# Attention feeding two mixture layers on one core: probabilities turned on VectorE and stored in runs of 32 words, a longer landing time in the written-out order, and the small block's last second products untied

## The chip, the cores and the metric

The kernel runs on one core of one Trainium2 chip. A core has five engines that matter here, each with its own in-order instruction stream: TensorE (PE, with its weight loads PEld), VectorE (DVE), ScalarE (ACT), GpSimd (POOL) and SyncE (SP), which issues nearly all DMAs. The metric is the device time of one execution in microseconds (us); lower is better.

## The reference

```python
q_s = softmax(q, axis=-1); k_s = softmax(k, axis=2)       # 1e-9 added to each sum; q, k, v: [4, 8, 576, 64] float32
attn = einsum('bhsd,bhde->bhse', q_s, einsum('bhsd,bhse->bhde', k_s, v))
x = attn.transpose(0, 2, 1, 3).reshape(2304, 512)
h = x @ w_in                                              # w_in: 512 x 2048, 64-bit floats
g = where(h >= 1, h, where(h <= -1, 0, (h + 1)**2 / 4))
x = g @ w_out                                             # w_out: 2048 x 512, 64-bit floats
p = probs / (probs.sum(-1) + 1e-9)                        # probs: [2304, 4]
out = sum over e of p[:, e] * (relu(x @ w1[e]) @ w2[e])   # w1: [4, 512, 1024], w2: [4, 1024, 512]
```

## The kernel before

**Arithmetic.** Every float32 operand of a large product is split into a high half (a rounded copy, made by `split`, line 479 on ACT or 481 on DVE) and a low half (the rest, line 484 on POOL or DVE). A product of 128 x 512 outputs is three matmuls (`products`, lines 1114 to 1116): low x high, high x low, high x high. I call these three "one product".

**Blocks and passes.** The 2304 tokens are five blocks of 512, 512, 512, 256 and 512. Pass 0 works on blocks 1 and 0, pass 1 on blocks 2 and 4 and on the small block 3. Each pass runs the first layer (kind "a": w_in, w_out) and then the four experts (kind "b": w1, w2), in weight chunks of 128 columns. `ups` emits the first products of a chunk (into `ups_banks`), `gated` or `opened` turns them into the gate (in pass 0, kind "a": lines 1539, 1543 and 1545, on DVE, ACT and DVE), and `downs` emits the second products (into `out_banks`). For pairs of full blocks the products follow Strassen's scheme, with sums of operands in place of the eighth product. In pass 1 the pairs' second products are `second_pairs`; their results are added in `add_pair` (line 1666), combined by `finish_pairs` (`total`), turned by TensorE (line 1718), copied and stored by `turned` (line 1704). The small block's second products are plain ones; `finish_expert` (line 1749) weights them with the probabilities and adds them.

**Probabilities.** `norm_probs` loads the 2304 x 4 probabilities with 36 small DMAs (line 512), normalizes them on DVE (lines 517 to 520), and writes those of blocks 2 and 4 to a DRAM tile `rows_of_p` of 4 rows x 1024, one row for each expert, in 8 DMAs that transpose on the way (line 530). `load_p` (line 469) reads a row of it back, broadcast over 128 partitions, for each expert of pass 1.

**What sets the order.** Each piece of work is a Python generator; `Order.run` simulates the engines with a table of costs and due times and emits the instructions in the order in which that simulation starts them. On the chip each engine then keeps that order, whatever the real times are. `arrival` is the simulation's estimate of when a DMA has landed: a start, the bytes at 360 GB/s, and 0.9 us. DMAs use eight completion counters in turn, and SP issues a DMA only when the last one on the same counter has landed.

Of the kernel before, what the change touches and what calls it, by code (L numbers as in the profile page):

```python
# [8 lines left out]
F32 = mybir.dt.float32  # L9
# [8 lines left out]
P = 128  # L18
# [46 lines left out]
class Order:  # L65
# [6 lines left out]
    HOP = 0.2  # L72
    SPAN = 40.0
# [79 lines left out]
    def arrival(self, issued, size):  # L153

        self.dma_free = max(issued + 0.45, self.dma_free) + size * P / 360e3
        return self.dma_free + 0.9
# [42 lines left out]
def attention_moe_kernel(  # L199
# [48 lines left out]
    CARE = 0.1  # L248
    GATE_DUE = 1
# [14 lines left out]
    def used(g, j):  # L264

        bi, ws = groups[g]
        return (*ws[j], PASS_OF[bi])
# [31 lines left out]
    pn = const.tile([P, NT // P, NE], F32, name="pn")  # L299
    psum_p = const.tile([P, NT // P], F32, name="psum_p")  # L300
# [204 lines left out]
    def norm_probs():  # L505
        start = Event()
        start.set(150.0)
        yield start
        for i in range(NT // P):
            for o, n, rows in token_rows(probs, i * P, P):  # L510
                t = yield SP, 0.65
                nc.sync.dma_start(out=pn[o:o + n, i, :], in_=rows)
        late = Event()
        late.set(t + 3)
        yield late
        t = yield dve(300)
        nc.vector.tensor_reduce(out=psum_p, in_=pn, axis=AX.X, op=ALU.add)
        nc.vector.tensor_scalar(out=psum_p, in0=psum_p, scalar1=EPS, scalar2=None, op0=ALU.add)
        nc.vector.reciprocal(out=psum_p, in_=psum_p)
        nc.vector.tensor_tensor(  # L520
            out=pn, in0=pn, in1=psum_p.unsqueeze(2).to_broadcast([P, NT // P, NE]), op=ALU.mult
        )
        probs_in.set(t)
        i0 = blocks[PASSES[1][0][0]][0] // P
        at = 0
        for bi in PASSES[1][0]:
            b0, n = blocks[bi]
            for i in range(n // P):
                t = yield SP, 0.65
                nc.sync.dma_start(  # L530
                    out=rows_of_p[:, at:at + P].rearrange("e p -> p e"), in_=pn[:, b0 // P + i, :]
                )
                at += P
        rows_in.set(t + 5)
# [135 lines left out]
    def second_of(w):  # L670
        return [u[:, 512:] for u in slot_of[w]] if w[0] == "a" and not is_kept(w) else [
            slot_of[w][:, z * 512:(z + 1) * 512] for z in range(2)]
# [564 lines left out]
    def ups():  # L1237
        for s, (g, j) in enumerate(steps):
# [3 lines left out]
            if w[0] == "b" or is_kept(w):  # L1242
                i, kind = w[3], w[0]
                pair, rest = PASSES[i]
                if bi == pair[0] and j % 2 == 0:
# [8 lines left out]
                    if kind == "b" and i:  # L1254
                        order.care = CARE
# [302 lines left out]

    def downs():
        s0 = 0  # L1560
        for g, (bi, ws) in enumerate(groups):
            n, kind, nj = blocks[bi][1], ws[0][0], len(ws)
# [7 lines left out]
            m = KC if kind == "a" else n // P  # L1570
            place = order_of[bi, kind]
            each = [(j, c) for j in range(nj) for c in range(m)]
            if kind == "a" and bi == PASSES[0][0][1] and g == place[-1]:

                each = [x for x in each if x[0] < 2] + [(j, c) for c in CORDER for j in range(2, nj)]
            ps, left, begun = {}, [m] * nj, [0] * m
            for j, c in each:
                w = used(g, j)
                if left[j] == m:
                    yield s0 + j  # L1580
                    yield ready[w, 1]
                    yield hidden[g, j]
                _, gh, gl = gate_of[g, j]
                bh, bl = second_of(w)
                first, last = begun[c] == 0, begun[c] == nj - 1
                begun[c] += 1
                if first:
                    ps[c] = yield out_banks[c]
                cs = slice(c * P, (c + 1) * P)
                t = yield pe(n if kind == "a" else DM, 3)  # L1590
                if kind == "a":
                    products(ps[c][:, :n], bh[:, cs], bl[:, cs], gh, gl, first, last)
                else:
                    products(ps[c], gh[:, cs], gl[:, cs], bh, bl, first, last)
                if last:
                    order.add((finish_first if kind == "a" else finish_expert)(
                        bi, w, c, ps[c], g == place[0], g == place[-1]), "ffn")
                left[j] -= 1
                if not left[j]:
                    for x in gate_of.pop((g, j))[0]:  # L1600
                        give_gate(x, t)
                    if step_of[w][1] == s0 + j:
                        x = slot_of.pop(w)
                        for x in x if isinstance(x, tuple) else (x,):
                            units.put(x, t)
# [67 lines left out]
    def finish_pairs():  # L1673
# [33 lines left out]
        for c in range(2):  # L1707
            order.add(total(c), "ffn", len(steps))
        for bi, which in ((b2, (1, 3)), (b1, (0, 2))):
            for k in range(blocks[bi][1] // P):  # L1710
# [10 lines left out]
                order.add(turned(bi, k, bank), "ffn", len(steps))  # L1721

    def finish_first(bi, w, c, p, first, last):
# [10 lines left out]
        out_banks[c].put(p, t)  # L1734
# [3 lines left out]
    def finish_expert(bi, w, c, p, first, last):  # L1738
# [13 lines left out]
        out_banks[c].put(p, t)  # L1752
# [11 lines left out]
    with tc.manual_schedule():  # L1764
# [18 lines left out]
        order.add(finish_pairs(), "ffn", len(steps))  # L1783
# [36 lines left out]
```

## Time and profile before

| what | value |
|---|---|
| time, median of 3 runs | 1262.95 us (1262.72 to 1267.39) |
| the profiled execution: its own time | 1272.47 us |
| its span, first to last instruction | 1270.7 us |
| mean granted TensorE clock | 0.984 |
| PE busy | 1219.2 us, 96% of the span |
| DVE, POOL, ACT busy | 820.0, 730.2, 519.8 us |
| chain that ended last | PE 82%, DVE 6%, DMA 5% |

The profiled execution is 9.5 us longer than the median of the runs. Its views are read with its own time in mind. A busy PE counts a matmul that is issued at the lower clock as busy too, so what PE loses is its idle time and what a low granted clock costs.

### The profile page before, as it was taken

The numbers are of one execution on the slowest core, as the hardware profiler recorded it, in microseconds if no ns is written. First come the engines' busy times: TensorE is split into PE (matmuls) and PEld (weight loads), VectorE is DVE, ScalarE is ACT, GpSimd is POOL, SyncE is SP. The second block draws the span as 40 slices with busy tenths as digits, with TensorE's granted clock in tenths as the row PEclk, the third lists the DMA queues.
The fourth block names the chain that finished last, engine by engine and source line by source line (L and its number), as shares of the span: only waits on it lengthen the run. The fifth ranks groups of instructions, "written<-read, shape, count | busy, mean of one in ns | idle before, by whom it ended". The sixth has DMA issues, their size and how long they took to land.

```text
span 1270.7 us, 16472 instructions
## 1 busy us (share of the span) xinstructions
PE 1219.2 (96%) x5802; PEld 1006.3 (79%) x5802; DVE 820.0 (65%) x1246; ACT 519.8 (41%) x957; POOL 730.2 (57%) x680
## 2 busy tenths in 40 slices
PE   9989999599999999999999999999999999999996
PEld 6868888467878778888788888887888888888885
DVE  5977783366655665444651735658777787787786
ACT  4667654343544434332454433625232232233221
POOL 2413231648788878776666737423675576566652
PEclk9989999799999999999999999999999999999999
DMA  8656659316556543534283221513234433443312
GB/s 230 197 176 241 200 200 50 127 41 199 170 191 198 169 157 127 179 126 144 70 258 102 68 86 48 166 51 130 103 133 145 137 133 116 148 135 110 115 42 83
DMA packets 109458, 174.67 MB, mean 137 GB/s; under 512 B 34880, under 2 KB 67648, under 8 KB 109376
## 3 DMA queue, kind: packets, MB, share of 16 engines
q1 hardware_dynamic: 108576, 172.31, 44.6%
q10 hardware_dynamic: 800, 1.31, 0.3%
q8 instruction: 46, 0.75, 0.3%
q14 instruction: 36, 0.29, 0.1%
HBM read 118.53 MB, written 55.07 MB: 137 GB/s over the span
## 4 chain that ended last, share of the span: by engine, by line
PE 82%; DVE 6%; DMA 5%; ACT 2%; issue 2%; POOL 1%; SPq 1%; ACTq 0%; DVEq 0%; POOLq 0%
PE bank L1115 26%; PE bank L1114 26%; PE bank L1116 26%; DMA rows_of_p<-pn 1%; DMA words<-in_moe_w_dram 1%; PE bank L975 1%; PE bank L1070 1%; DVE x L484 1%; PE bank L1109 1%; PE bank L1060 1%; DVE gate_late L484 1%; POOL w L484 1%; DMA w<-kept 1%; DMA acc<-in_k_dram 0%; DVE mk L914 0%
## 5 line engine op out<-in xcount | busy, mean ns | idle before, releaser
L1114 PE MATMUL bank<-x,w 128*128 128x512 f32 (+1 forms) x988 | 373.5, 378 | 21.5 <-DVE cv L1545 12.4
L1115 PE MATMUL bank<-x,w 128*128 128x512 f32 (+1 forms) x988 | 368.0, 372 | 5.6 <-DVE x L484 3.5
L1116 PE MATMUL bank<-x,w 128*128 128x512 f32 (+1 forms) x988 | 366.8, 371 | 0.0
L1114 PEld LDWEIGHTS bank<-x,w 128*128 128x128 f32 x988 | 187.4, 190 | 60.9 <-DVE cv L1545 13.3
L1115 PEld LDWEIGHTS bank<-x,w 128*128 128x128 f32 x988 | 187.7, 190 | 39.9 <-DVE x L484 6.0
L1116 PEld LDWEIGHTS bank<-x,w 128*128 128x128 f32 x988 | 187.5, 190 | 31.9
L484 POOL TENSOR_TENSOR w<-words,w 128x512 fp32r<-128x512 f32 (+1 forms) x112 | 137.2, 1237 | 89.8 <-ACT w L479 58.3
L1666 DVE TENSOR_TENSOR acc<-bank,acc 128x512 f32<-128x512 f32 x182 | 120.0, 686 | 23.2 <-PE bank L1116 23.2
L484 POOL TENSOR_TENSOR gate_late<-cv,gate_late 128x512 fp32r<-128x512 f32 (+1 forms) x68 | 88.5, 1309 | 75.2 <-ACT gate_late L479 74.8
L484 POOL TENSOR_TENSOR w<-cv,w 128x512 fp32r<-128x512 f32 x75 | 97.7, 1306 | 33.7 <-ACT w L479 31.6
L484 POOL TENSOR_TENSOR x<-cv,x 128x512 fp32r<-128x512 f32 x29 | 42.8, 1476 | 108.8 <-ACT x L479 91.9
L1114 PE MATMUL bank<-w,gate 128*128 128x512 f32 x240 | 98.3, 410 | 0.0
L479 ACT CAST gate_late<-cv 128x512 fp32r<-128x512 f32 (+1 forms) x80 | 47.8, 601 | 120.6 <-DVE cv L1441 86.3
L1115 PE MATMUL bank<-gate_late,w 128*128 128x512 f32 (+1 forms) x248 | 94.7, 382 | 2.1 <-DVE gate_late L484 1.8
L1114 PE MATMUL bank<-gate_late,w 128*128 128x512 f32 (+1 forms) x248 | 94.1, 379 | 2.1 <-DVE acc L1733 2.1
L1116 PE MATMUL bank<-w,gate 128*128 128x512 f32 x240 | 94.5, 394 | 0.0
L1115 PE MATMUL bank<-w,gate 128*128 128x512 f32 x240 | 94.4, 393 | 0.0
L1116 PE MATMUL bank<-gate_late,w 128*128 128x512 f32 (+1 forms) x248 | 93.8, 378 | 0.0
L479 ACT CAST w<-words 128x512 fp32r<-128x512 f32 (+1 forms) x120 | 68.4, 591 | 54.2 <-DMA words<-in_moe_w_dram 30.0
L1749 DVE SCALAR_TENSOR_TENSOR acc<-bank,pn,acc 128x512 f32<-128x512 f32 x70 | 49.4, 749 | 52.2 <-PE bank L1116 52.2
L484 POOL TENSOR_TENSOR gate<-cv,gate 128x512 fp32r<-128x512 f32 (+1 forms) x44 | 53.8, 1228 | 47.9 <-ACT gate L479 47.9
L1115 PE MATMUL bank<-gate,w 128*128 128x512 f32 (+1 forms) x188 | 70.4, 375 | 2.9 <-POOL gate L484 2.8
(227 smaller groups left out, 2303.3 us busy)
## 6 DMA issues: line engine op xcount, KB each, us to landing
words<-in_moe_w_dram SPq DMA_DIRECT2D x64, 512.0 KB, 4.3
sums<-w SPq DMA_DIRECT2D x64, 512.0 KB, 4.9
w<-sums SPq DMA_DIRECT2D x64, 512.0 KB, 4.5
kept<-w SPq DMA_DIRECT2D x32, 512.0 KB, 4.9
w<-kept SPq DMA_DIRECT2D x32, 512.0 KB, 4.3
words<-in_moe_w_in_dram SPq DMA_DIRECT2D x16, 512.0 KB, 4.7
words<-in_moe_w_out_dram SPq DMA_DIRECT2D x16, 512.0 KB, 6.0
wide<-in_k_dram SPq DMA_DIRECT2D x20, 160.0 KB, 5.4
```

The source lines that it names most:

```text
L479: nc.scalar.copy(out=dst, in_=src)
L484: (nc.vector if engine == DVE else nc.gpsimd).tensor_tensor(**kw)
L975: nc.tensor.matmul(bank[:, :N], ek[:, c, :], vt_buf[:, c * N:(c + 1) * N], start=(c == 0), stop=(c == NC - 1),)
L1060: nc.tensor.transpose(bank[:, i * P:i * P + m], eq[:m, c], ident[:m, :m])
L1070: nc.tensor.matmul(bank[:, :hi - lo], bd, qt_buf[:, lo:hi], start=True, stop=True)
L1109: nc.tensor.matmul(bank[:, :P], ident, ident, start=True, stop=True)
L1114: nc.tensor.matmul(ps, al, bh, start=first, stop=False, **kw)
L1115: nc.tensor.matmul(ps, ah, bl, start=False, stop=False, **kw)
L1116: nc.tensor.matmul(ps, ah, bh, start=False, stop=last, **kw)
L1666: nc.vector.tensor_tensor(out=dst, in0=p, in1=dst, op=ALU.add)
L1749: nc.vector.scalar_tensor_tensor(out=dst, in0=p, scalar=by, in1=dst, op0=ALU.mult, op1=ALU.add)
```

## The change

There are three edits that act, and names for numbers that stay.

1. `norm_probs` copies the normalized probabilities of blocks 2 and 4 into a 128 x 32 tile, turns it on VectorE in squares of 32 x 32, and writes it with 4 DMAs, each of 32 runs of 32 words. Before, 8 DMAs wrote 512 single words each.
2. The constant at the end of `arrival` is 1.9 us in place of 0.9 (`LANDING`).
3. `downs` is divided: its body becomes `group_downs`, and the last group (the small block's last expert) is added as a work item of its own, from the banks of `ups`, due 8 steps later (`REST_LATER`), so that it is no longer bound to follow the pairs' second products. `finish_pairs` and its parts come due 8 steps earlier (`END`).

`CARE1` and `CARE2` are 1, which is the value that held there before. Where the program is written out with `END` at 0 and all else as changed, every engine's order is the same as with 8, so `END` moves nothing.

```diff
@@ Order
     HOP = 0.2
+    LANDING = 1.9
...
     def arrival(self, issued, size):
         self.dma_free = max(issued + 0.45, self.dma_free) + size * P / 360e3
-        return self.dma_free + 0.9
+        return self.dma_free + self.LANDING
@@ norm_probs
         probs_in.set(t)
-        i0 = blocks[PASSES[1][0][0]][0] // P
-        at = 0
-        for bi in PASSES[1][0]:
-            b0, n = blocks[bi]
-            for i in range(n // P):
-                t = yield SP, 0.65
-                nc.sync.dma_start(
-                    out=rows_of_p[:, at:at + P].rearrange("e p -> p e"), in_=pn[:, b0 // P + i, :]
-                )
-                at += P
+        yield dve(100)
+        for k, bi in enumerate(PASSES[1][0]):
+            i0, m = blocks[bi][0] // P, blocks[bi][1] // P
+            nc.vector.tensor_copy(
+                out=p_cols[:, k * m * NE:(k + 1) * m * NE].rearrange("p (i e) -> p i e", e=NE),
+                in_=pn[:, i0:i0 + m, :],
+            )
+        yield dve(64)
+        nc.vector.transpose(out=p_rows, in_=p_cols)
+        for r in range(P // 32):
+            t = yield SP, 0.65
+            nc.sync.dma_start(
+                out=rows_of_p.rearrange("e (i r j) -> i e r j", r=P // 32, j=32)[:, :, r],
+                in_=p_rows[r * 32:(r + 1) * 32],
+            )
         rows_in.set(t + 5)
@@ ups
-                    if kind == "b" and i:
-                        order.care = CARE
+                    order.care = {("b", 0): CARE1, ("a", 1): CARE2, ("b", 1): CARE}[kind, i]
@@ downs: the body of its loop is now group_downs(g, s0, banks, later)
+            if g == len(groups) - 3:
+                order.add(group_downs(g + 2, s0 + 2 * nj, ups_banks, REST_LATER), "ffn",
+                          s0 + 2 * nj + REST_LATER)
...
+            if g < len(groups) - 1:
+                yield from group_downs(g, s0)
@@ group_downs
-                    yield s0 + j
+                    yield s0 + j + later
...
-                    ps[c] = yield out_banks[c]
+                    ps[c] = yield (out_banks[c] if banks is None else banks)
@@ second_pairs, finish_pairs: total and turned
-            order.add(total(c), "ffn", len(steps))
+            order.add(total(c), "ffn", len(steps) - END)
```

**How the order moves.** With the first edit alone the order differs only at its own instructions: the 4 DMAs in place of the 8, and three more on DVE. Here is SP at that place, between the last `kept` stores of the first layer and the first expert's weights (`words`). Before:

```order
L828 DMA kept_1590<-w_93 128x1024
L530 DMA rows_of_p<-pn 128x4x1 x8
L828 DMA kept_1667<-w_94 128x1024
L828 DMA kept_1667<-w_95 128x1024
L606 DMA words<-in_moe_w_dram 128x4x256
L606 DMA words<-in_moe_w_dram 128x2x512
```

and of the change (a number behind a name is the buffer's own, two higher now because there are two new tiles; line 606 is now 618, 828 is 840):

```order
L840 DMA kept_1599<-w_95 128x1024
L542 DMA rows_of_p<-p_rows 8x4x32 x4
L840 DMA kept_1675<-w_96 128x1024
L840 DMA kept_1675<-w_97 128x1024
L618 DMA words<-in_moe_w_dram 128x4x256
L618 DMA words<-in_moe_w_dram 128x2x512
```

The neighbours are the same. With all three edits, PE, DVE, ACT and POOL too keep their order of before from here on until about 250 us of the trace of before.

The second edit moves work in two stretches: in the attention of batches 0 and 1 (on PE up to about 90 us of the trace of before, on DVE up to 160), and in the first experts, where the attention of batches 2 and 3 is mixed in (about 280 to 510 us). Elsewhere few neighbours change places, and from pass 1 on almost none. This is DVE early in the program, where the second weight chunk of the first layer (`words_118`, `m`) is converted beside the attention. Before:

```order
L1044 TENSOR_REDUCE sq_168<-wide_135 128x10
L1046 TENSOR_SCALAR sq_168<-sq_168 128x10
L1047 RECIPROCAL sq_168<-sq_168 128x10
L982 TENSOR_SCALAR rk_154<-bank_124 128x2
L985 RECIPROCAL rk_154<-rk_154 128x2
L1008 TENSOR_REDUCE mq_169<-wide_137 128x10
L1083 TENSOR_TENSOR x_77<-bank_127,x_75 128x64
```

and of the change:

```order
L1056 TENSOR_REDUCE sq_170<-wide_137 128x10
L1058 TENSOR_SCALAR sq_170<-sq_170 128x10
L1059 RECIPROCAL sq_170<-sq_170 128x10
L819 SCALAR_TENSOR_TENSOR m_121<-words_120,m_121 128x1024
L1095 TENSOR_TENSOR x_79<-bank_127,x_77 128x64
L1095 TENSOR_TENSOR x_75<-bank_127,x_73 128x256
L994 TENSOR_SCALAR rk_156<-bank_128 128x2
```

Line 819 (807 before) is a step of that conversion. It stood 26 rows further down before, behind the attention work. On PE, 27 of the first layer's products now stand ahead of the last attention product of batch 1 (line 1070), where 23 did.

The third edit moves PE's work near the end. Before, at the last expert (`gate_late_3718` and `3719` are the halves of one gate operand of the pairs; the small block's products have the gate on the right):

```order
L1116 MATMUL bank_122<-x_71,w_104 128x256
L1114 MATMUL bank_124<-gate_late_3718,w_101 128x512
L1115 MATMUL bank_124<-gate_late_3719,w_101 128x512
L1116 MATMUL bank_124<-gate_late_3718,w_101 128x512
L1114 MATMUL bank_125<-gate_late_3718,w_101 128x512
L1115 MATMUL bank_125<-gate_late_3719,w_101 128x512
```

and of the change:

```order
L1128 MATMUL bank_125<-x_73,w_107 128x256
L1126 MATMUL bank_131<-w_95,gate_late_3792 128x512
L1127 MATMUL bank_131<-w_95,gate_late_3792 128x512
L1128 MATMUL bank_131<-w_95,gate_late_3792 128x512
L1126 MATMUL bank_130<-w_95,gate_late_3792 128x512
L1127 MATMUL bank_130<-w_95,gate_late_3792 128x512
L1128 MATMUL bank_130<-w_95,gate_late_3792 128x512
L1126 MATMUL bank_131<-w_103,gate_late_3793 128x512
L1127 MATMUL bank_131<-w_103,gate_late_3793 128x512
L1128 MATMUL bank_131<-w_103,gate_late_3793 128x512
L1126 MATMUL bank_126<-gate_1700,w_96 128x512
```

Three of the small block's eight last products now stand ahead of the pairs' products that follow their last first products; one more stands among those, and four behind them. Before, all eight stood behind. On DVE the two weightings (line 1749) now stand ahead of two of the three last sums of `total` that DVE makes.

## Rows read from the trace of the kernel before

**Rows 1.** Windows: us, busy time (instructions) of PE, PEld, DVE, ACT, POOL; granted clock; DMA share; GB/s.

```profile
500.00:600.00 100.00, 100.00 (x443) 82.79 (x442) 44.27 (x65) 32.58 (x60) 72.57 (x75) 1.00 0.44 153
```

**Rows 2.** Windows of 5 us around the first experts' start.

```profile
205.00:210.00 5.00, 5.00 (x24) 4.14 (x23) 0.69 (x1) 1.69 (x4) 2.59 (x2) 1.00 1.95 0
...
225.00:230.00 5.00, 0.00 (x0) 0.00 (x0) 0.00 (x0) 0.62 (x1) 0.56 (x1) 0.75 1.00 335
230.00:235.00 5.00, 0.24 (x1) 0.24 (x2) 0.99 (x2) 2.38 (x4) 4.92 (x6) 0.50 0.08 26
...
240.00:245.00 5.00, 5.00 (x13) 3.89 (x14) 0.61 (x1) 0.62 (x1) 2.86 (x3) 0.54 0.44 153
```

**Rows 3.** Timeline of PE there: start, duration, line, operation [idle before, releaser].

```profile
221.93 0.39 PE L1116 MATMUL bank<-x,w 128*128 128x512 f32 x1
234.76 0.79 PE L1114 MATMUL bank<-x,w 128*128 128x512 f32 x1 [12.44 <-DVE cv L1545]
...
239.75 0.80 PE L1115 MATMUL bank<-x,w 128*128 128x512 f32 x1 [1.72 <-POOL x L484]
...
244.61 0.40 PE L1114 MATMUL bank<-gate,w 128*128 128x512 f32 x1
```

**Rows 4.** Timelines of DVE and ACT there.

```profile
216.99 0.69 DVE L1539 TENSOR_SCALAR cv<-bank 128x512 f32<-128x512 f32 x1 [10.20 <-PE bank L1116]
234.01 0.69 DVE L1545 TENSOR_TENSOR cv<-bank,cv 128x512 f32<-128x512 f32 x1 [16.33 <-ACT cv L1543]
...
228.75 0.62 ACT L479 CAST w<-words 128x512 fp32r<-128x512 f32 x1 [21.25 <-DMA words<-in_moe_w_dram]
...
233.26 0.72 ACT L1543 ACTIVATE cv<-cv,half 128x512 f32<-128x512 f32 x1
```

**Rows 5.** Timeline of SP there: its DMA issues.

```profile
194.38 4.45 SPq L530 DMA_DIRECT2D rows_of_p<-pn  x8
...
212.15 9.17 SPq L606 DMA_DIRECT2D words<-in_moe_w_dram  x3
```

**Rows 6.** Waits of SP, 185 to 300 us: total, times, longest.

```profile
SPq L828 <- DMA rows_of_p<-pn: 12.4, 1, 12.4
```

**Rows 7.** DMA issues of the whole run: count, KB each, median us to landing.

```profile
words<-in_moe_w_dram SPq DMA_DIRECT2D x64, 512.0 KB, 4.3
...
pn<-in_moe_domain_probs_dram SPq DMA_DIRECT2D x36, 1.0 KB, 3.1
...
rows_of_p<-pn SPq DMA_DIRECT2D x8, 2.0 KB, 26.5
```

**Rows 8.** The tile `rows_of_p`: where it is read (issue ns, first and last start).

```profile
L469 SPq DMA_DIRECT2D acc<-rows_of_p x4: 338/598/1029, 644.5 to 1041.8; - x4
```

**Rows 9.** Timeline of DVE, 193 to 203 us.

```profile
194.12 0.23 DVE L520 TENSOR_TENSOR pn<-pn,psum_p 128x72 f32<-128x72 f32 x1
...
197.91 1.22 DVE L807 SCALAR_TENSOR_TENSOR m<-words,m 128x1024 int32<-128x1024 int32 x1
...
201.01 1.28 DVE L818 SCALAR_TENSOR_TENSOR w<-x,t 128x1024 fp32r<-128x1024 f32 x1
```

**Rows 10.** Window at the end of batch 1's attention.

```profile
65.00:85.00 20.00, 15.73 (x70) 12.12 (x68) 15.49 (x24) 13.71 (x26) 3.69 (x6) 0.83 0.45 143
```

**Rows 11.** A stop of PE in the first experts, and the window after it.

```profile
468.86 0.50 PE L1114 MATMUL bank<-x,w 128*128 128x512 f32 x1 [2.37 <-DVE gate L1513]
...
470.00:480.00 10.00, 10.00 (x38) 7.80 (x37) 6.28 (x12) 4.71 (x8) 5.01 (x5) 0.83 0.13 49
```

**Rows 12.** Timelines of PE, DVE and ACT's DMA issues at the end.

```profile
1246.57 0.50 PE L1115 MATMUL bank<-gate_late,w 128*128 128x512 f32 x1 [1.75 <-DVE gate_late L484]
...
1257.62 2.78 PE L1718 MATMUL bank<-ident,acc 128*128 128x128 f32 x24
...
1257.14 1.44 DVE L1749 SCALAR_TENSOR_TENSOR acc<-bank,pn,acc 128x512 f32<-128x512 f32 x2 [0.30 <-PE bank L1116]
...
1264.23 3.32 ACTq L1704 DMA_DIRECT2D out_dram<-cv  x4
```

More of the change, by code (lines that the diff above doesn't have):

```diff
@@ L248, in attention_moe_kernel @@
     CARE = 0.1
+    CARE1 = 1
+    CARE2 = 1
+    END = 8
+    REST_LATER = 8
     GATE_DUE = 1
@@ L299, in attention_moe_kernel @@
     pn = const.tile([P, NT // P, NE], F32, name="pn")
+    p_cols = const.tile([P, 32], F32, name="p_cols")
+    p_rows = const.tile([P, 32], F32, name="p_rows")
     psum_p = const.tile([P, NT // P], F32, name="psum_p")
@@ L1557, in gated, with group_downs @@
         hidden[g, j].set(t + MARGIN)
+    def group_downs(g, s0, banks=None, later=0):
+        bi, ws = groups[g]
+        n, kind, nj = blocks[bi][1], ws[0][0], len(ws)
+        m = KC if kind == "a" else n // P
+        place = order_of[bi, kind]
+        each = [(j, c) for j in range(nj) for c in range(m)]
+        if kind == "a" and bi == PASSES[0][0][1] and g == place[-1]:
+            each = [x for x in each if x[0] < 2] + [(j, c) for c in CORDER for j in range(2, nj)]
+        ps, left, begun = {}, [m] * nj, [0] * m
+        for j, c in each:
+            w = used(g, j)
+            if left[j] == m:
+                yield s0 + j + later
+                yield ready[w, 1]
+                yield hidden[g, j]
+            _, gh, gl = gate_of[g, j]
+            bh, bl = second_of(w)
+            first, last = begun[c] == 0, begun[c] == nj - 1
+            begun[c] += 1
+            if first:
+                ps[c] = yield (out_banks[c] if banks is None else banks)
+            cs = slice(c * P, (c + 1) * P)
+            t = yield pe(n if kind == "a" else DM, 3)
+            if kind == "a":
+                products(ps[c][:, :n], bh[:, cs], bl[:, cs], gh, gl, first, last)
+            else:
+                products(ps[c], gh[:, cs], gl[:, cs], bh, bl, first, last)
+            if last:
+                order.add((finish_first if kind == "a" else finish_expert)(
+                    bi, w, c, ps[c], g == place[0], g == place[-1],
+                out_banks[c] if banks is None else banks), "ffn")
+            left[j] -= 1
+            if not left[j]:
+                for x in gate_of.pop((g, j))[0]:
+                    give_gate(x, t)
+                if step_of[w][1] == s0 + j:
+                    x = slot_of.pop(w)
+                    for x in x if isinstance(x, tuple) else (x,):
+                        units.put(x, t)
     def downs():
@@ L1561, in downs @@
         for g, (bi, ws) in enumerate(groups):
-            n, kind, nj = blocks[bi][1], ws[0][0], len(ws)
+            nj = len(ws)
+            if g == len(groups) - 3:
+                order.add(group_downs(g + 2, s0 + 2 * nj, ups_banks, REST_LATER), "ffn",
+                          s0 + 2 * nj + REST_LATER)
             if is_paired(used(g, 0)) and bi in PASSES[used(g, 0)[3]][0]:
@@ L1569, in downs @@
                 continue
[L1570 to L1579, printed above, removed]
-                    yield s0 + j
[L1581 to L1587, printed above, removed]
-                    ps[c] = yield out_banks[c]
[L1589 to L1605, printed above, removed]
+            if g < len(groups) - 1:
+                yield from group_downs(g, s0)
             s0 += nj
@@ L1720, in finish_pairs, with finish_first @@
                     )
-                order.add(turned(bi, k, bank), "ffn", len(steps))
-    def finish_first(bi, w, c, p, first, last):
+                order.add(turned(bi, k, bank), "ffn", len(steps) - END)
+    def finish_first(bi, w, c, p, first, last, banks):
         n = blocks[bi][1]
@@ L1733, in finish_first, with finish_expert @@
             nc.vector.tensor_tensor(out=dst, in0=p[:, :n], in1=dst, op=ALU.add)
-        out_banks[c].put(p, t)
+        banks.put(p, t)
         if last:
             y_in[bi, c].set(t)
-    def finish_expert(bi, w, c, p, first, last):
+    def finish_expert(bi, w, c, p, first, last, banks):
         i = blocks[bi][0] // P + c
@@ L1751, in finish_expert @@
             )
-        out_banks[c].put(p, t)
+        banks.put(p, t)
         if last:
@@ L1782, in attention_moe_kernel @@
         order.add(gate_operands(), "ffn")
-        order.add(finish_pairs(), "ffn", len(steps))
+        order.add(finish_pairs(), "ffn", len(steps) - END)
         order.add(load_p(), "load")
```

## The prediction

> **What bounds the kernel now.** I read the totals first: PE is busy for 96% of the span, and the chain that ended last is PE for 82%. So a change gains only what PE stands idle or runs slowly. The windows show PE's full rate: 443 matmuls in 100 us without a gap, 0.2257 us each [rows 1]. Then I looked, window by window, for stretches with fewer. The largest lies at 222 to 245 us [rows 2]: from 225 to 230 PE issues nothing, and from 240 to 245, busy throughout, it issues 13 matmuls at a granted clock of 0.54, about its lower level of 1.2 GHz, after the idle stretch. Between the last matmul before the stop, at 221.93, and the first one at full pace again, at 244.61, stand 15 matmuls [rows 3], which shows the two ends and two of them. They take 15 x 0.2257 = 3.4 us at full rate; from 222.16 (221.93 plus one step) to 244.61 are 22.45 us. The stop costs 22.45 - 3.4 = 19.05 us.
>
> Why PE stops is read backwards. PE waits at 234.76 for a bank that DVE frees at line 1545 [rows 3]. DVE has stood 16.33 us in front of that instruction, waiting for ACT's square (line 1543), whose input DVE made at 216.99 [rows 4]. ACT does the square only at 233.26, because in its in-order stream the cast of the first expert's weights stands ahead, and that cast waited 21.25 us, until 228.75, for the DMA of `words`. SP issued that DMA at 212.15 [rows 5]; before it SP had stood 12.4 us in front of a `kept` store, waiting for a `rows_of_p` DMA [rows 6]. The 8 `rows_of_p` DMAs were issued at 194.38, carry 2 KB each and land after 26.5 us in the median, where 512 KB of `words` take 4.3 [rows 7]. Meanwhile DMA engines are busy at a share of 1.95 with nothing to show in GB/s [rows 2]. So 16 KB in 4096 single words hold up the weights, and the in-order ACT passes that on to PE.
>
> **Edit 1, the probabilities.** It removes the 4096 single-word writes and adds 128 writes of 32 words in 4 DMAs. Their cost is in no row. Per piece, the old ones took from 194.38 to about 221, some 27 us for 4096: 128 pieces would take under 1 us. From above: if bytes set it, the same 16 KB take the same 27 us. The nearest row is the load of the probabilities, DMAs of 64 short pieces, which land after 3.1 us [rows 7]; it is a load and not a store, yet nothing there lasts tens of us. I take 3 us, off the path, since SP does not wait for them before it needs their counters again eight DMAs later, and they are read first at 644.5 us [rows 8].
>
> Then SP reaches the `kept` stores when their input is there: DVE's line 818 ends at 201.01 + 1.28 = 202.3 [rows 9]. With two stores at some 0.4 us each, `words` is issued at about 203.6 and lands, with 4.3 us [rows 7], at 207.9. ACT came to its cast at 228.75 - 21.25 = 207.5 [rows 4], so it waits 0.4 us in place of 21.25. The casts up to the square took 233.26 - 228.75 = 4.5 us, so ACT is ready at 212.4, before DVE's 216.99 + 0.69 = 217.68. Square 0.72, line 1545 0.69: the bank is free at 219.1, while PE gets there at 222.16. It does not wait. What could remain is the gate's low half: in the trace PE got it at 239.75, 5.05 us after line 1545 ended at 234.70 [rows 3, 4]; from 219.1 that would be 224.2, where PE wants it four matmuls after 222.16, at 223.07. So 0 to 1.1 us remain; I take 0.6, as part of those 5.05 us was POOL catching up on weights. Edit 1 gains 19.05 - 0.6 = 18.4 us, at most 19.05; at least, if the new stores clog as long, nothing.
>
> On DVE it adds two copies and a transpose. The nearest row is 0.23 us for 72 columns [rows 9], so 0.7 us together; DVE is busy for 0.69 us of 5 from 205 to 210 [rows 2], which hides them. Without that cover they would cost 0.7. Behind them stands the first layer's last weight conversion, which has that slack.
>
> The Trainium skill ("DMA: Bandwidth & Descriptors", Specifications) puts the smallest transfer for full rate at 512 bytes and says that below it the DMA engine reads, modifies and writes. Runs of 32 words are 128 bytes, so by that rule alone the new stores stay in the slow class, and the sum could fall to the bytes' price above; the same page (Rules for kernel authors) says that a non-contiguous last dimension lowers to one descriptor per element, by which 32 times fewer pieces go. The 26.5 us for 2 KB agree with both; which of them sets the price, no row shows.
>
> **Edit 2, the landing time.** It adds no instruction; it reorders. In the attention, line 807 (1.22 us) of the second weight's conversion and its followers (818: 1.28 us) [rows 9] move ahead on DVE, and four more products stand ahead of batch 1's last attention product: 4 x 3 x 0.2257 = 2.7 us of PE work moved to where PE stands idle. From 65 to 85 us it is busy 15.73 of 20 at a granted clock of 0.83 [rows 10]: 4.3 us idle and 15.73 x 0.17 = 2.7 us of pace, so at most 7.0 to gain. The moved conversion steps, if they all fell on attention's path, would cost 1.22 + 1.28 and a step between them that is shorter than either: at most 3.8 us. I take a gain of 2, somewhat under the 2.7 moved. In the first experts it may remove the stop at 468.86, 2.37 us and then a window with 38 matmuls in 10 us, 10 - 38 x 0.2257 = 1.4 us lost: 3.8 together [rows 11]; or make one like it. PE waited there for a gate, not for a DMA, so I take zero.
>
> **Edit 3, the tail.** Before, PE waits 1.75 us for the pairs' last-but-few gate operand [rows 12]. Now two products that are ready (6 x 0.2257 = 1.35 us) stand ahead of it, and a third whose gate comes just behind that operand on DVE: the hole shrinks by about 1 us. Given back: the weightings (1.44 us) now stand on DVE ahead of sums that the turning of the output (PE from 1257.62) waits for, and ACT's output DMAs, which end the program, follow from there. Bounds: a gain of 1.75, a loss of 1.44; I take a gain of 0.5. `END` moves nothing.
>
> **Sum.** 18.4 + 2 + 0.5 = 20.9 us off the profiled execution's own 1272.47 (1.8 us around its span): 1251.6. But that execution is 9.5 us over the runs' median of 1262.95. If the excess lies in the clogged stretch (profiling small DMA pieces may lengthen it, which no row shows), the runs have only 8.9 us of that stop to give, and the change comes out at 1262.95 - 11.4 = 1251.6; if it lies elsewhere, at 1262.95 - 20.9 = 1242.05. Nothing decides, so I take the middle, 1247.
>
> **Rivals.** *The stores still clog* (the bytes' price): ACT waits on as before, and only edits 2 and 3 act, 1262.95 - 2.5 = 1260.5. For it: the pieces stay short. Against: the 64-piece loads of 3.1 us [rows 7]. Chance 0.07; by the rule on 512 bytes this would be the outcome.
>
> *New stops in the first experts*: one to three like that at 468.86, at 3.8 us each [rows 11], give 1251 to 1258, say 1254.5. For it: ACT and POOL are reordered there thoroughly, and each engine keeps the planned order whatever happens. Against: the planned landing comes nearer to 4.3 us, so the order waits less on chip. Chance 0.20.
>
> *More than I take*: the stop at 65 to 85 us goes whole (7.0 in place of 2) and the excess lies elsewhere: 1242 - 5 = 1237. Chance 0.12.
>
> *Slower*: weight pairs come late throughout the first experts, because the order puts attention's POOL work ahead of their conversion. There are 16 pairs in pass 0's experts, about nine of them in the reordered stretch. To reach 1269.3, 0.5% over the median, from 1247 takes 22.3 us, six such stops of 3.8: six of nine pairs. Chance 0.05, at 1270. Against it stands POOL's share, 73% from 500 to 600 [rows 1], which leaves time to catch up.
>
> **Numbers.** The forecast, 1247 with 1241 to 1252 for itself, holds 0.56. Half a per cent, 6.3 us, is about what a measurement of this kernel tells from none; the line lies at 1256.6. Faster: 0.56 + 0.12 + 0.14 of the new stops = 0.82; same: 0.07 + 0.06 = 0.13; slower 0.05. For 8 in 10 I reach from half of the 1237 case to the three-stop case: 1237 to 1258.
>
> **What would show it.** After: no PE window near 205 to 230 us under 20 matmuls in 5 us, and the granted clock at 1.00 there; ACT's cast of the first expert's `words` waiting under 2 us; `rows_of_p` landing in a few us; PE's wait at the last expert under 1 us. The prediction is wrong if the stop stays with `words` late (the stores), if PE stops there for something else than `words`, or if the windows between 280 and 510 us count fewer matmuls than before.

## The result, and the profile after

The changed kernel takes 1249.59 us in the median of 4 runs (1249.13 to 1250.96). The kernel before, beside it, has 1265.17 (1262.72 to 1267.9, 4 runs). The ratio is 0.9878, with a 95% interval of 0.985 to 0.9906: 1.2% faster. The profiled execution takes 1249.13 us (span 1247.3) against 1272.47, which is 23.3 us less.

The same views as before, of the changed kernel. The totals, and the windows that answer to [rows 2]:

```profile
PE 1211.3 (97%) x5816; PEld 1003.9 (80%) x5816; DVE 821.2 (66%) x1245; ACT 521.6 (42%) x958; POOL 736.7 (59%) x683
...
205.00:210.00 5.00, 5.00 (x23) 4.13 (x23) 2.76 (x4) 4.94 (x9) 2.59 (x2) 1.00 0.51 199
225.00:230.00 5.00, 5.00 (x24) 4.14 (x23) 2.77 (x4) 2.55 (x6) 3.89 (x4) 1.00 0.44 160
230.00:235.00 5.00, 5.00 (x24) 4.14 (x23) 2.56 (x4) 2.30 (x4) 2.43 (x2) 1.00 0.13 52
240.00:245.00 5.00, 5.00 (x24) 4.14 (x23) 2.77 (x4) 2.77 (x6) 4.33 (x5) 1.00 0.26 105
```

The stop is gone whole: 23 or 24 matmuls in each window, the granted clock at 1.00, and the DMA engines at a share of 0.51 with 199 GB/s where they had 1.95 with nothing. SP, ACT and DVE at that place, answering to [rows 4 to 6]:

```profile
200.25 2.88 SPq L542 DMA_DIRECT2D rows_of_p<-p_rows  x4
206.65 1.31 SPq L840 DMA_DIRECT2D kept<-w  x2
208.02 3.02 SPq L618 DMA_DIRECT2D words<-in_moe_w_dram  x3
...
213.97 0.62 ACT L486 CAST w<-words 128x512 fp32r<-128x512 f32 x1 [1.15 <-DMA words<-in_moe_w_dram]
...
222.31 0.69 DVE L1550 TENSOR_SCALAR cv<-bank 128x512 f32<-128x512 f32 x1 [10.20 <-PE bank L1128]
223.79 0.69 DVE L1556 TENSOR_TENSOR cv<-bank,cv 128x512 f32<-128x512 f32 x1 [0.79 <-ACT cv L1554]
```

ACT waits 1.15 us for `words` in place of 21.25, and DVE 0.79 for the square in place of 16.33. But the gate step of line 1539 (now 1550) comes at 222.31, where it came at 216.99: up to there the change has lost 5.3 us. Where they go shows further ahead, in PE's and POOL's timelines and SP's:

```profile
85.00 2.54 PE L987 MATMUL bank<-acc,wide 128*128 128x130 f32 x10 [3.96 <-POOL wide L981]
...
84.57 0.12 POOL L980 MEMSET acc<- 128x10 f32 x1 [8.63 <-DMA acc<-in_v_dram]
...
73.57 0.56 SPq L618 DMA_DIRECT2D words<-in_moe_w_in_dram  x1
74.18 0.50 SPq L618 DMA_DIRECT2D words<-in_moe_w_out_dram  x1
74.78 1.30 SPq L840 DMA_DIRECT2D kept<-w  x2
76.49 0.83 SPq L976 DMA_DIRECT2D acc<-in_v_dram  x1
```

PE waits for POOL, and POOL for a load of `v`, which SP issued behind 1 MB of weights and 1 MB of `kept` stores. In before the stores stood ahead of two loads of `v` there, where they now stand ahead of four:

```profile
70.25 1.21 SPq L964 DMA_DIRECT2D wide<-in_v_dram  x2
71.55 2.57 SPq L828 DMA_DIRECT2D kept<-w  x2
74.17 1.51 SPq L964 DMA_DIRECT2D wide<-in_v_dram  x2
```

That is not the only link. The four loads ahead of those weights are late as well (issued from 70.93, in before from 63.60): SP stood 10.1 us in front of the first, waiting for DVE, where it stood 6.1 us in before (waits of SP, 59 to 72 us of the changed kernel and 57 to 70 us of before):

```profile
SPq L976 <- DVE acc L491: 10.1, 1, 10.1
```

```profile
SPq L964 <- DVE x L1083: 6.1, 1, 6.1
```

And later PE waits for a converted weight, in all nine profiles planned with 1.9 and in none of the five whose start is planned with 0.9:

```profile
129.43 0.50 PE L1126 MATMUL bank<-x,w 128*128 128x512 f32 x1 [1.22 <-DVE w L830]
```

The window of the changed kernel that answers to [rows 10] has lost busy time, though not clock:

```profile
65.00:85.00 20.00, 14.43 (x75) 10.69 (x74) 17.65 (x31) 12.24 (x27) 1.90 (x5) 0.97 0.57 156
```

At the end, answering to [rows 12]: PE does not wait at the last expert any more, but 1.22 us for DVE ahead of the output's turning.

```profile
1235.55 2.52 PE L1740 MATMUL bank<-ident,acc 128*128 128x128 f32 x21 [1.22 <-DVE acc L491]
...
1233.46 1.44 DVE L1771 SCALAR_TENSOR_TENSOR acc<-bank,pn,acc 128x512 f32<-128x512 f32 x2 [0.23 <-PE bank L1128]
```

**A ledger.** Three stretches make up every span: from the start to the gate step at 216.99 [rows 4] (G); from there to a DVE step behind the stop that all kernels share, the next to last of its kind there, at 276.66 in before (S); and from S to the span's end. Here it is for all profiles, the experiments too (us; each worked out from the two rows and the span). Landing is that of the plan.

| kernel | edits | landing | start to G | G to S | S to end |
|---|---|---|---|---|---|
| before | none | 0.9 | 216.99 | 59.67 | 994.04 |
| changed | 1, 2, 3 | 1.9 | 222.31 | 40.58 | 984.41 |
| e1 | 1 | 0.9 | 219.55 | 40.60 | 987.65 |
| e2 | 2 | 1.9 | 222.38 | 57.59 | 986.03 |
| e3 | 1, 3 | 0.9 | 218.78 | 40.59 | 987.13 |
| e4 | 1, 2 | 1.9 | 220.69 | 40.56 | 989.45 |
| e5 | all, 4096 words more | 1.9 | 220.39 | 56.07 | 986.04 |
| e6 | all, 1024 words more | 1.9 | 222.31 | 40.59 | 986.40 |
| e7 | all, 1024 short runs more | 1.9 | 221.16 | 40.59 | 987.95 |
| e8 | all, 4096 words by ACT | 1.9 | 220.41 | 53.76 | 986.53 |
| e9 | none, stores spread | 0.9 | 217.19 | 48.03 | 1014.58 |
| e10 | all, landing late | 0.9, then 1.9 | 215.58 | 40.65 | 987.27 |
| e11 | all, 4096 runs of 32 more | 1.9 | 220.84 | 40.58 | 987.78 |
| e12 | all, 4096 far words more | 1.9 | 221.09 | 40.58 | 988.13 |

The middle column without a stop is 40.6 in every kernel; what is above it is the stop: 19.1 us in before.

### The profile page after: what moved, and what is told of

Its sections match the earlier page's. It is cut to its first block, busy times and chain, and to the rows that moved or that the text cites. A ratio compares the mean times of both kernels' runs of the same rounds, so it can differ in the third digit from the quotient of the medians.

```text
span 1247.3 us, 16496 instructions
## 1 busy us (share of the span) xinstructions
PE 1211.3 (97%) x5816; PEld 1003.9 (80%) x5816; DVE 821.2 (66%) x1245; ACT 521.6 (42%) x958; POOL 736.7 (59%) x683
## 2 busy tenths in 40 slices
DMA packets 105394, 174.67 MB, mean 140 GB/s; under 512 B 30816, under 2 KB 63584, under 8 KB 105312
## 4 chain that ended last, share of the span: by engine, by line
PE 89%; DVE 6%; ACT 1%; issue 1%; POOL 1%; DMA 1%; ACTq 0%; SPq 0%; POOLq 0%; DVEq 0%
PE bank L1127 28%; PE bank L1126 28%; PE bank L1128 27%; PE bank L987 2%; PE bank L1121 1%; PE bank L1082 1%; DVE x L491 1%; PE bank L1072 1%; DMA acc<-in_v_dram 1%; DVE gate L491 1%; DVE gate L1524 0%; POOL w L491 0%; DVE gate_late L491 0%; DVE acc L491 0%; DVE mk L926 0%
## 5 line engine op out<-in xcount | busy, mean ns | idle before, releaser
L491 POOL TENSOR_TENSOR gate<-cv,gate 128x512 fp32r<-128x512 f32 (+1 forms) x60 | 76.8, 1284 | 69.8 <-ACT gate L486 69.4
L491 POOL TENSOR_TENSOR gate_late<-cv,gate_late 128x512 fp32r<-128x512 f32 (+1 forms) x53 | 67.0, 1269 | 59.3 <-ACT gate_late L486 57.7
L1126 PE MATMUL bank<-w,gate 128*128 128x512 f32 x220 | 89.7, 408 | 0.0
L1126 PE MATMUL bank<-gate,w 128*128 128x512 f32 (+1 forms) x224 | 84.0, 375 | 2.1 <-DVE acc L1755 2.1
L1128 PE MATMUL bank<-w,gate 128*128 128x512 f32 x220 | 86.0, 391 | 0.0
L1127 PE MATMUL bank<-w,gate 128*128 128x512 f32 x220 | 85.8, 390 | 0.0
L1127 PE MATMUL bank<-gate,w 128*128 128x512 f32 (+1 forms) x224 | 84.5, 377 | 0.3
L1128 PE MATMUL bank<-gate,w 128*128 128x512 f32 (+1 forms) x224 | 83.8, 374 | 0.0
L486 ACT CAST gate<-cv 128x512 fp32r<-128x512 f32 (+1 forms) x70 | 41.7, 599 | 94.8 <-DVE cv L1452 65.4
L1127 PE MATMUL bank<-gate_late,w 128*128 128x512 f32 (+1 forms) x212 | 79.6, 375 | 0.2
```

Source lines behind the costliest of these rows:

```text
L486: nc.scalar.copy(out=dst, in_=src)
L491: (nc.vector if engine == DVE else nc.gpsimd).tensor_tensor(**kw)
L1126: nc.tensor.matmul(ps, al, bh, start=first, stop=False, **kw)
L1127: nc.tensor.matmul(ps, ah, bl, start=False, stop=False, **kw)
L1128: nc.tensor.matmul(ps, ah, bh, start=False, stop=last, **kw)
```

## Experiments

### One edit more or less: e1 to e4

e1 is before with edit 1; e2 is before with `LANDING` 1.9. The other two are the changed kernel with one thing back:

```diff
-    LANDING = 1.9
+    LANDING = 0.9
```

for e3, and for e4 the last group inside the one task:

```diff
-            if g == len(groups) - 3:
-                order.add(group_downs(g + 2, s0 + 2 * nj, ups_banks, REST_LATER), "ffn",
-                          s0 + 2 * nj + REST_LATER)
...
-            if g < len(groups) - 1:
-                yield from group_downs(g, s0)
+            yield from group_downs(g, s0)
```

e1: 

> Before, with edit 1 alone (probabilities turned on DVE, 4 stores of 32 runs of 32 words). Theory A: the single-word stores alone made the stop at 222 to 245 us, so the stop is gone whole and this kernel holds nearly all of the gain: its profile shows the first gate step behind the first layer at 217 us as before, full windows from 220 to 245, and the timed runs are 14 to 19 us under before. Rival B: the profiler stretched the clogged stores, and the timed runs have only about 9 us of that stop to give. Rival C: in the changed kernel the stop vanished because of the longer landing time (the weights' place in the order); then this kernel still stops there and stays within 3 us of before.

e2: 

> Before, with edit 2 alone (landing time 1.9 in place of 0.9). Theory A (from the pair of traces): the attention at the start gets longer by about 5 us, and the first experts and the second pass's first layer give back 3 to 6; the stop behind the single-word stores stays, some 19 us. Together within 3 us of before. Rival (the prediction's term): the start gains 2 us, the kernel is 2 us faster, and the 5 us at the start were one execution's own. Rival D: the planned landing alone moves the weights so that the stop is gone: 14 us or more faster.

e3: 

> The changed kernel, with the landing time back at 0.9. Theory A: the first gate step behind the first layer comes at 217 us and not at 222, what the start wins is given back in the first experts (about 3 us) and near 660 us of before (about 3), so the time is within 3 us of the changed kernel. Rival: the landing time is worth its 2 us or more, and this kernel is slower by that. Rival E: the start's 5 us are the landing time's and nothing is given back: 5 us faster than the changed kernel.

e4: 

> The changed kernel, with the small block's last second products back in the one task (edit 3 undone). Theory A: all is as in the changed kernel up to its last 30 us; PE again waits 1 to 2 us for the pairs' gate at the last expert, and the whole is 1 to 2 us slower than the changed kernel. Rival: the hole is filled but the end of the program, set by the output's turning and its DMAs, moves by less than 0.5 us; no difference.

| kernel | median us (lowest to highest, runs) | ratio to before |
|---|---|---|
| before, same chip | 1269.15 (1261.68 to 1275.07, 17) | |
| e1 | 1249.59 (1248.25 to 1249.86, 4) | 0.984 (0.9815 to 0.9866) |
| e2 | 1268.27 (1262.89 to 1277.24, 12) | 1.0007 (0.9983 to 1.0031) |
| e3 | 1248.09 (1246.8 to 1250.43, 5) | 0.9833 (0.9806 to 0.9859) |
| e4 | 1252.76 (1249.28 to 1255.79, 6) | 0.9869 (0.9845 to 0.9893) |

**Edit 1 is the whole gain**: 1269.15 - 1249.59 = 19.6 us alone. Rivals B (9 us in the runs) and C fall: e2 keeps the stop at 17.0 us. e1's profile shows the cast with almost no wait:

```profile
205.25 2.30 SPq L613 DMA_DIRECT2D words<-in_moe_w_dram  x3
...
210.47 0.62 ACT L481 CAST w<-words 128x512 fp32r<-128x512 f32 x1 [0.41 <-DMA words<-in_moe_w_dram]
```

**Edit 2 costs.** Start to G is 215.6 to 219.6 us in the five profiles whose start is planned with 0.9, mean 217.6, and 220.4 to 222.4 in the nine with 1.9, mean 221.3: 3.7 us, without an overlap. Behind S nothing clear is given back: with edit 3, 986.8 in the mean of the eight profiles with 1.9 there (e10 among them), against 987.1 (e3). In the runs e4 is 3.2 us over e1. e2 alone does not show the cost: its ratio's interval reaches from 2.2 us faster to 3.9 slower, and its stop is 2.1 us shorter than that of before. For e3, the expected 3 us given back did not come; nor was it 5 us faster: it is 1.5 below the changed kernel, which was not measured beside it.

**Edit 3 gains** 1.3 to 1.9 us by two pairs of single profiles; in the runs e3 is 1.5 us under e1. A DVE step of pass 1 comes at the same time in e1 and e3:

```profile
812.75 1.37 DVE L1740 TENSOR_TENSOR acc<-bank,acc 128x512 f32<-128x512 f32 x2 [5.25 <-PE bank L1123]
```

```profile
812.76 1.37 DVE L1755 TENSOR_TENSOR acc<-bank,acc 128x512 f32<-128x512 f32 x2 [5.25 <-PE bank L1128]
```

The first is e1's, the second e3's. From there e1 needs 1247.8 - 812.75 = 435.05 us and e3 1246.5 - 812.76 = 433.74. With the longer landing the same step stands at 815.39 in e4 and at 813.90 in the changed kernel, so 435.31 and 433.40: e4 is 1.9 us slower there, as its theory A has it; its runs are 3.2 over the changed kernel's, which were not measured beside them. In e1 the old hole is where it was:

```profile
1223.94 0.50 PE L1122 MATMUL bank<-gate_late,w 128*128 128x512 f32 x1 [1.75 <-DVE gate_late L486]
```

### What makes the single words slow: e5 to e8, e11, e12

Each is the changed kernel with 4 more stores behind its own 4, into a spare tile (e5: 128 x 32 x 2 words, so that the words lie 8 bytes apart; in before they lay 4 bytes apart):

```diff
+        for r in range(P // 32):
+            rows = slice(r * 32, (r + 1) * 32)
+            nc.sync.dma_start(out=spare[rows, :, 0], in_=p_rows[rows])
```

e8 is the same, issued by ACT (`nc.scalar`). e12 has a spare tile of 128 x 32 x 128, so that the words lie 512 bytes apart. e6 writes 8 words of each row, `p_rows[rows, :8]`, again 8 bytes apart. e7 writes each row as 8 runs of 4 words, 32 bytes apart. e11 writes each row of 32 words 32 times, as runs of 128 bytes that lie 256 bytes apart.

e5: 

> The changed kernel, with 4 more stores behind its own four, that write the same 16 KB once more to a spare tile as 4096 single words (the output stays the reference's). Theory pieces: the chip pays by the piece, 27 us for 4096 as before; the stop comes back, some 15 to 20 us in the profile, PE idle near 230 us, ACT's cast of the first expert's words waiting 15 us or more. Theory layout: the old stores were slow because their words came from 128 partitions of a tile of normalized probabilities, 4 words each; from the turned tile single words cost no more than runs, and the time is that of the changed kernel within 2 us.

e6: 

> As e5, with a quarter of it: 4 stores of 256 single words, 4 KB in all. Theory pieces: 1024 of 4096, some 7 us of clog; the first expert's words are issued 2 to 4 us later than in the changed kernel, which ACT's slack hides: no stop, time within 2 us of the changed kernel. Theory bytes: the same, a quarter of the bytes and some 7 us. It is the pair to e7, which has the same pieces and four times the bytes.

e7: 

> As e5, with the 16 KB in 1024 runs of 4 words. Theory pieces: like e6, some 7 us of clog and no stop. Theory bytes (runs under some length all pay by their bytes): like e5, some 27 us, with the stop. Landing of these stores: about a quarter of that of e5 by pieces, the same by bytes.

e8: 

> As e5, but the 4 stores of single words are issued by ACT. Theory shared engines: the words of the first expert are held up in the DMA engines themselves, behind the single words, whoever issued those; SP issues them at about 208 us as in the changed kernel, they land near 225 to 230, and a stop of 10 to 18 us stays. Theory counters: what cost the time was SP standing in front of a store until a counter came free; without it the words land at about 214 and there is no stop.

e11: 

> As e5, with 4096 runs of 32 words each in the 4 added stores, 512 KB in all in place of 16. Theory pieces: like e5, a stop of 13 to 17 us in the profile, 1261 to 1268 us. Theory short words: only pieces of a word or a few are slow; runs of 128 bytes pass like other transfers of 512 KB, in about 4 us each, and the time is within 4 us of the changed kernel. Theory bytes: 32 times the bytes cost more than e5; above 1275 us.

e12: 

> As e5, with the 4096 single words 512 bytes apart from each other in the spare tile. Theory neighbours: single words were slow because many went into the same short stretch of memory; here each has its own, they land in a few us, and the time is within 3 us of the changed kernel. Theory pieces: like e5, 1261 to 1268 us, landing 15 us in the median.

Their rows in the view of DMA issues (count, KB each, median us to landing), in the order e5, e6, e7, e8, e11, e12:

```profile
spare<-p_rows SPq DMA_DIRECT2D x4, 4.0 KB, 15.5
```

```profile
spare<-p_rows SPq DMA_DIRECT2D x4, 1.0 KB, 3.4
```

```profile
spare<-p_rows SPq DMA_DIRECT2D x4, 4.0 KB, 2.5
```

```profile
spare<-p_rows ACTq DMA_DIRECT2D x4, 4.0 KB, 16.1
```

```profile
spare<-p_rows SPq DMA_DIRECT2D x4, 128.0 KB, 2.7
```

```profile
spare<-p_rows SPq DMA_DIRECT2D x4, 4.0 KB, 5.3
```

| kernel | median us (runs) | ratio to before | stop (G to S, less 40.6) |
|---|---|---|---|
| e5: 4096 words, 8 bytes apart | 1264.17 (10) | 0.9978 (0.9955 to 1.0) | 15.5 |
| e6: 1024 words, 8 bytes apart | 1251.66 (4) | 0.9882 (0.9837 to 0.9928) | none |
| e7: 1024 runs of 4 words | 1250.15 (4) | 0.9866 (0.9811 to 0.992) | none |
| e8: e5's stores by ACT | 1259.61 (10) | 0.9955 (0.993 to 0.9981) | 13.2 |
| e11: 4096 runs of 32 words | 1251.69 (4) | 0.9865 (0.9841 to 0.9888) | none |
| e12: 4096 words, 512 bytes apart | 1250.31 (4) | 0.9856 (0.9831 to 0.9881) | none |

The stop is made at will: e5 brings it back from the turned tile, so the old layout in SBUF is not needed for it. e7 refutes a price by the bytes: e5's 16 KB in runs of 4 words land in 2.5 us. e6 and e7 fit both a price by the piece and one by closeness; that e6's pieces would delay the issue of the first expert's words by 2 to 4 us did not come (208.02 in e6, as in the changed kernel). e11 refutes the piece: as many pieces as in e5 and 32 times the bytes land in 2.7 us. The packets say that they are as many, e5 first, e11 second; the changed kernel has 30816 under 512 bytes.

```profile
DMA packets 109554, 174.69 MB, mean 138 GB/s; under 512 B 34976, under 2 KB 67744, under 8 KB 109472
```

```profile
DMA packets 109554, 175.20 MB, mean 140 GB/s; under 512 B 34976, under 2 KB 67744, under 8 KB 109472
```

e12 changes one thing against e5, the distance of the words in memory, and they land in 5.3 us in place of 15.5, without a stop. So single words that lie close together are what costs; far apart they still take twice e11's time. The Trainium skill ("DMA: Bandwidth & Descriptors", Specifications) puts all transfers under 512 bytes in one class, in which the DMA engine reads, modifies and writes; e11's runs of 128 bytes do not behave like e5's words, so here the class is not one.

e5 and e8 also settle how the words reach PE. In e5 SP does not stand in front of `kept` for a counter and issues the expert's words at 207.30, as early as in the changed kernel; ACT still waits until 229.66:

```profile
204.74 2.51 SPq L844 DMA_DIRECT2D kept<-w  x2
207.30 2.72 SPq L622 DMA_DIRECT2D words<-in_moe_w_dram  x3
...
229.66 0.62 ACT L487 CAST w<-words 128x512 fp32r<-128x512 f32 x1 [18.75 <-DMA words<-in_moe_w_dram]
...
235.67 0.79 PE L1130 MATMUL bank<-x,w 128*128 128x512 f32 x1 [9.95 <-DVE cv L1560]
```

In e8, where ACT issues the stores, SP issues the words at 207.81 and the cast starts at 227.36:

```profile
207.81 7.22 SPq L622 DMA_DIRECT2D words<-in_moe_w_dram  x3
...
227.36 0.62 ACT L487 CAST w<-words 128x512 fp32r<-128x512 f32 x1 [14.75 <-DMA words<-in_moe_w_dram]
```

What is held is what both queues share, and not SP's queue. This agrees with the Trainium skill ("DMA: Bandwidth & Descriptors", Rules for kernel authors), by which issuing from another engine gives no other DMA engines. While it lasts, the DMA engines are busy and move little, in e5 a share of 0.95 at 40 GB/s; whether they are slow themselves or the memory behind them, no run here shows:

```profile
215.00:220.00 5.00, 5.00 (x24) 4.14 (x23) 0.00 (x0) 0.00 (x0) 0.00 (x0) 1.00 0.95 40
```

### The old stores, spread out: e9

```diff
                 t = yield SP, 0.65
+                gap = Event()
+                gap.set(t + 40)
                 nc.sync.dma_start(
...
                 at += P
+                yield gap
```

> Before, with its 8 stores of 512 single words each left as they are, but planned 40 us apart, so that only the first stands ahead of the first expert's words; every other engine keeps its order of before. Theory: the stop came from 4096 pieces at one place; 512 of them cost the DMA engines some 3 us, less than the slack of the loads behind them. The stop is gone and the time is that of edit 1 alone, 1248 to 1252 us. Rival: each of the eight holds up a load or a store that something waits for, 1 to 3 us each, and the time stays above 1256 us.

e9 takes 1279.05 us (1267.08 to 1281.55, 10 runs, three of them under 1272), ratio 1.0069 (1.0041 to 1.0096): slower than before. That is the rival's way, and further than its 1 to 3 us a store; the theory's 3 us for 512 words was wrong. The trace has the landing of three of the eight stores. One of 2 KB by itself takes 13.3 to 15.6 us, half of the burst's 26.5 and more for an eighth of its words (that 26.5 stands for the last two of the burst, the only ones whose landing the trace of before has). The view of the DMA issues, and below it that of the tile (least, median and most):

```profile
rows_of_p<-pn SPq DMA_DIRECT2D x8, 2.0 KB, 14.1
...
DMA to landing us min/median/max: 13.3/14.1/15.6
```

e5's first store, with twice the words, lands in 6.8 us:

```profile
DMA to landing us min/median/max: 6.8/15.5/22.7
```

So by the word the old stores are dearer than e5's. In them the words that lie side by side in memory come from neighbouring partitions, in e5 from one partition, and they lie 4 bytes apart in place of 8; which of these counts, or the loads in flight beside them, no run shows.

Loads issued beside such a store land late. The first still makes a stop of 48.03 - 40.6 = 7.4 us. Behind others stand these waits of PE; the waits of ACT for weights are one behind the first store (216.57) and one behind the fifth (388.03):

```profile
304.46 0.47 PE L920 MATMUL bank<-ident,mk 128*128 128x128 f32 x1 [6.60 <-DVE mk L917]
...
390.53 0.77 PE L1117 MATMUL bank<-x,w 128*128 128x512 f32 x1 [5.65 <-DVE gate L1516]
...
216.57 0.62 ACT L479 CAST w<-words 128x512 fp32r<-128x512 f32 x1 [8.86 <-DMA words<-in_moe_w_dram]
...
388.03 0.62 ACT L479 CAST w<-words 128x512 fp32r<-128x512 f32 x1 [9.86 <-DMA words<-in_moe_w_dram]
```

SP itself stood 13.6 us once, in front of a store of `sums`, for a `rows_of_p` landing, so a part of the loss may pass through its queue. Spread out, the same 4096 words cost more than in one burst.

### The longer landing time behind the start only: e10

```diff
-        return self.dma_free + self.LANDING
+        return self.dma_free + (self.LANDING if issued > 120 else 0.9)
```

> The changed kernel, with the landing time 0.9 for what is planned in the first 120 us and 1.9 behind: PE's order is that of the kernel with 0.9 throughout up to the end of the first two batches' attention. Theory: the longer landing time costs about 3 us at the start (the last loads of v behind a weight chunk's stores) and gives back 1 to 2 later; this kernel keeps only the second: 1245 to 1247 us, faster than both. Rival: what is given back later is chance of single executions; the time is that with 0.9 throughout, 1248 us, within 1 us.

e10 takes 1247.81 us (1243.48 to 1249.65, 5 runs), ratio 0.9834 (0.9808 to 0.986). That is e3's 1248.09 within the scatter: the rival holds, and the longer landing has nothing to give behind the start that these runs can show. e3 and e10 are the fastest kernels of the study, 1.5 to 1.8 us under the changed one, which is little more than the runs scatter.

## Why the prediction was right, and where its steps were off

**The forecast**, 1247 us, lies 2.6 under the 1249.59 measured, inside its own range. The sign, the place and the main term were right. That it came so near is in part luck: edit 2 came out 5.7 us worse than its term, and edit 1 (0.7), edit 3 (about 1.1) and the excess of the profiled execution (4.75 taken by the halving, some 5.9 by what these terms leave over) gave half of that back.

**Edit 1** was put at 18.4 us off the profile. It is 59.67 - 40.60 = 19.1, the whole stop: the 0.6 us kept back for the gate's low half did not appear. The steps up to the cast hold: a wait of 0.4 us forecast, 0.41 in e1. That the two agree is luck: 202.3 and two stores of 0.4 are 203.1 and not 203.6, by which ACT would not wait at all, and in e1 the words took 210.47 - 205.25 = 5.2 us and not 4.3. Two reasons given for it fall. The price was reckoned by the piece ("128 pieces would take under 1 us", and 3 us were taken); e11 shows 4096 pieces that make no stop and land in 2.7 us a store, and e12 that closeness of single words is what counts. And SP's 12.4 us in front of the `kept` store were told as a link of the chain; in e5 that link is missing and the words land as late.

**Profile and median.** The forecast halved the 9.5 us by which the profiled execution lay above the median, because that could be the profiler's work on small pieces. It was mostly the three runs that were low: beside the experiments, 15 to 19 runs of before have medians of 1265.83 to 1269.15, and edit 1 alone takes 19.6 us off. Nor does the profiler seem to stretch the stop: e5's is 15.5 us in the profile, and its runs are 14.6 over the changed kernel's. The profiled execution had excess elsewhere too. From S to the end it took 994.04 us, e1 in the same order 987.65; of these 6.4 us, 5.1 are three windows like that in [rows 11], each 10 x (1 - 0.83) = 1.7 us, at 470, 620 and 820 us. After the same wait of 2.07 us near 820 the clock fell in before and in e4, and stayed at 1.00 in the changed kernel and e1; why is open. How much of the scatter of before (1261.68 to 1275.07) is the stop's own size, 17.0 to 19.1 in the two profiles, and how much the clock, stays open too.

**Edit 2** was put at a gain of 2 us with a loss of 3.8 as the bound; it is a loss of 3.7. The step that failed is that products moved ahead fill PE's idle time: PE's wait there only changes its cause. The order also puts a weight chunk's stores ahead of two more loads of `v`; the prediction counted what the order moves on DVE and PE, and not what it moves on SP. But SP's 10.1 us in front of the loads before them are a wait for DVE, on which the conversion steps moved ahead; that fits the case that the bound of 3.8 was for. PE's 1.22 us at 129.43, for a converted weight, is in neither term. No run parts these links, so how the 3.7 us divide among them is open. For the first experts zero was taken, and nothing clear came.

**Edit 3** was put at 0.5 and measured 1.3 to 1.9. The hole of 1.75 us closed whole, where about 1 was taken, and 1.22 us of wait ahead of the output's turning were given back, where at most 1.44 were feared. That leaves 0.5; where the rest comes from is not shown.

**The rivals.** The stores do not clog; new stops in the first experts did not come. The rival of more than is taken, and the slower one, stayed away.

**What was to show it.** No window under 20 matmuls, ACT's wait under 2 us (1.15), PE's wait at the last expert under 1 (none): all as said. From 280 to 510 us PE has 1040 matmuls where before had 1020, so that sign of being wrong stayed away. For the landing of the 4 new stores the view has no time; e11's, of the same run length, take 2.7 us.

## What to carry to other kernels

Look for stores whose destination is written in single words that lie close together, even when they are few bytes: here one of 2 KB took 14 us, loads issued beside it came late, and an in-order engine passed the delay on to one that has nothing to do with it. Not every such store costs time: e6's 1024 words made no stop. Turn such data on chip and write runs. Issuing the stores from another engine left 13.2 of 15.5 us of stop, and spreading them made the kernel slower. When an order is planned anew, follow the loads on SP too: which stores they now stand behind, and which buffers they wait for.

## What the runs showed of the hardware that was not expected

- Single words 8 bytes apart land in 15.5 us and 512 bytes apart in 5.3 (4 stores of 1024 words each), while 4 stores of 1024 runs of 128 bytes, 32 times the bytes, land in 2.7.
- One store of 512 single words by itself took 13.3 to 15.6 us, the last two of eight at once 26.2 and 26.9. The price is not proportional to their number.
- After the same wait of 2.07 us the granted clock fell in one execution (before, 0.83 from 820 to 830 us) and not in another whose order is the same there (e1, 1.00).
